# Last two scatters issued together, the low halves of w1 last in each tile's products, two loads of w2 after the transposes, and more products of zeros early

## The chip, the cores and the metric

One core of one Trainium2 chip runs the kernel. The metric is device microseconds (us) of one execution. The engines are TensorE (PE, with its weight loads as PEld), VectorE (DVE), ScalarE (ACT), GpSimd (POOL) and SyncE (SP), which here only issues transfers.

## The reference, cut to what matters

Three layers run one after the other on 2 x 768 tokens of 384 numbers: a recurrent attention, a gated convolution network, and a mixture of eight experts. Only the last one is touched by most of the change:

```python
logits = x @ w_gate                      # which of 8 experts a token asks for
fresh  = argmax(logits)                  # a token takes it only if its local gate is < 0.5,
e      = fresh or the expert of the token before it
out[b, s] = p[e] * (relu(x[b, s] @ w1[e]) @ w2[e])      # w1: 384 x 1024, w2: 1024 x 384
```

## The kernel before, in words

Each engine's order is written out by hand. The string `SEQ` (L50 on) is a list of tokens; every token names a small generator and advances it by one `yield`, and what is emitted stands in that order in the queue of its engine. PE, DVE, ACT and SP keep it as written; POOL is tied to program order too. So a token that is moved changes what waits behind it on its engine.

Every fp32 matrix is split into two fp16 halves, a high one and a low one (w1 into `w1h` and `w1l`, w2 into `w2h` and `w2l`), and a product is three products: high x high, high x low, low x high (`PASSES`).

**Early.** PE begins with products of zeros, `warm` (token H, L235 to 240: 128x512 fp16, tile `psk`). H_1 and H_2 are the first 16, H_0 are 8 more after the first states `psu` (L397). Between them come the transposes of tables (`psT`, L305) and of the first keys (`ptf`, L326 and L341).

**Routing.** The twelve tiles of 128 tokens go through the second layer's output (`out_tile`, L660) and are scattered by POOL into `slots` in DRAM, one region for each expert (tokens S, `send`, L882). A row's place comes from the routing (`places_of`, tile `posb` for the last two tiles, `xrb` their rows). The first full tiles of the sorted list, U_0_0 to U_0_2, are known before the last two scatters: their rows are gathered first (`fetch`, tokens I, L956), transposed by a DMA from SP (`xsT<-yb`, L973) and multiplied. Then come scatters S_11 and S_10. Everything else reads `slots` after both: tiles with a fixed expert straight from there (`xsT<-slots`, L975), all others through gathers on POOL and transposes on SP.

**Experts, first half of w1 and w2 (phase 0).** Tokens W1_e_0 and W2_e_0 load 768 KB of an expert into one of three staging buffers `ws` from SP (L932, L946). ACT writes the high half (L498), and the low half is written by DVE (L155), or for the experts that `CFG['w1']` marks with `g` by POOL (three instructions L153, after ACT has scaled `ws` in place, L937, and cast it, L939). Experts 6, 5, 7, 3, 0, 4, 2, 1 come in this order. Tokens U are `up` (L1023): 9 products into `ph`, 18 for a tile of two halves. Where the expert is only known at run time, the weight is addressed by a register that PE loads from `ej`/`ejs` (L997, L1005), and a product of `w1l` then waits for the low halves of all experts. After `up` come relu and split (L1011, L1013), a transpose on PE (`pt`, L1041) or by DMA, and later D, `down` (L1052), whose result goes to the output by scatters of POOL.

`F` computes on DVE the row numbers for all later gathers (L856 to L878), BL_1 and BL_2 blank the gather buffers on DVE (L964 to L966), `M` opens the memory that w2 uses. SP also loads one register from `ej` (L1104) at a place that the builder chooses.

Of the kernel before, what the change touches and what calls it, by code (L numbers as in the profile page):

```python
# [50 lines left out]
C LD H_1 H_1 C WI_0 CV LD C C C C C C C H_2 H_2 C C T T LD LD LD T T WO_0 WI_3 T T WI_0 LD L_3 LD LD A_0 CV A_0 A_0 A_0 T A_0 A_1 T C WI_0 T WI_0 WO_0  # L51
WO_0 WI_2 A_1 A_1 A_1 CV CV B_0 C B_0 B_0 Y_0 CV Y_0 L_3 WO_0 B_0 Z_0 Z_0 H_0 H_0 Z_1 Z_0 L_2 GT B_1 Y_0 A_1 Y_0 A_1 A_1 Y_1 L_2 B_1 GT L_2 L_2 A_2
WI_3 WI_3 Y_0 A_2 A_2 GT Y_0 Y_1 A_2 A_2 WI_1 Z_1 Z_2 Y_1 Y_1 Z_2 A_2 A_2 Y_2 WI_3 WO_1 L_3 L_3 A_3 A_3 A_3 WO_0 Y_0 Y_1 B_1 B_1 WO_0 Z_3 WI_1 Z_1 Y_1
Y_1 B_2 WO_0 Y_2 A_3 Y_2 B_2 B_2 A_3 WI_1 A_3 A_3 L_4 L_4 L_4 L_4 L_7 Z_2 WI_1 Y_0 Y_2 Y_2 A_4 B_3 Y_1 Y_1 G_0_0_1 A_4 L_5 CV CV WO_0 WI_2 G_0_0_1 B_2
G_0_0_1 A_4 Y_2 A_4 Z_3 Y_3 CV G_0_0_1 Y_3 L_5 L_5 L_5 B_3 Y_3 Y_2 WO_0 WO_0 WI_2 WI_2 B_3 WO_0 G_0_0_1 B_3 WO_2 Z_4 G_0_0_1 B_4 G_0_0_0 Y_2 Y_2 Z_3
G_0_0_1 WO_0 G_0_0_1 G_0_0_2 G_0_0_1 WO_1 A_4 G_0_0_2 WO_0 WO_0 WO_0 G_0_0_0 A_4 A_4 Z_4 Y_3 A_5 A_5 A_5 A_5 L_6 G_0_0_2 WO_1 A_5 Y_4 Y_4 L_6 L_6 L_6
A_6 A_6 G_0_0_1 Y_3 B_4 G_0_0_2 G_0_0_2 A_5 A_5 WO_1 Y_3 WO_3 G_0_0_0 WO_1 Y_4 G_0_0_0 G_0_0_2 G_0_0_2 G_0_0_2 G_0_0_2 A_6 A_6 B_4 Z_4 Y_4 Y_4 G_0_0_2
G_0_0_2 Y_3 G_0_0_0 Y_3 L_7 WO_2 Y_3 WO_1 WO_1 WO_1 A_6 G_0_0_0 WO_1 G_0_0_0 G_0_0_0 B_4 Y_4 WO_2 Y_5 Y_5 G_0_0_2 L_7 L_7 G_0_1_2 A_7 Y_5 G_0_1_2
G_0_1_2 G_0_1_2 G_0_1_2 G_0_0_0 G_0_1_1 B_5 B_5 B_5 WO_1 WO_1 WO_1 WO_1 Y_5 Y_5 WO_1 WO_1 A_7 A_7 A_6 A_6 G_0_1_2 G_0_1_2 G_0_1_2 G_0_1_1 A_6 G_0_1_1
WO_2 G_0_0_0 B_6 L_8 WO_2 G_0_1_1 B_6 WO_2 Y_4 G_0_1_2 G_0_1_1 G_0_1_1 G_0_1_1 G_0_1_2 A_7 B_5 G_0_1_1 G_0_1_0 Y_4 G_0_1_0 A_6 A_6 Z_6 Z_6 L_10  # L60
G_0_1_2 B_6 G_0_1_0 G_0_1_0 G_0_1_0 WO_3 RC G_0_1_2 A_7 WO_2 L_8 WO_2 WO_2 G_0_1_1 WO_2 WO_2 G_0_1_1 A_7 Z_7 A_7 Y_6 Z_6 A_7 Y_5 G_0_1_3 WO_3 G_0_1_3
G_0_1_0 Y_6 Y_6 G_0_1_0 G_0_1_0 G_0_1_3 G_0_1_3 B_7 A_7 A_7 B_6 G_0_1_3 G_0_1_3 L_8 L_8 Y_5 Y_5 Y_5 G_0_0_3 G_0_0_3 Y_4 G_0_1_0 G_0_0_3 G_0_0_3
G_0_0_3 WO_2 WO_2 G_0_0_3 G_0_1_1 Y_6 WO_2 WO_2 L_9 L_9 Y_6 G_0_1_0 G_0_1_1 O_0_1 G_0_0_3 G_0_0_3 G_0_0_3 A_8 A_8 G_0_1_3 Z_7 B_7 G_0_0_3 B_7 WO_3
O_0_1 O_0_1 Y_7 WO_3 Y_7 G_0_2_0 G_0_0_3 G_0_0_3 A_8 G_0_2_0 G_0_1_3 G_0_2_0 Y_6 Z_7 G_0_1_3 Y_7 G_0_2_0 G_0_2_0 G_0_2_0 O_0_2 O_0_2 L_9 L_9 A_9 O_0_2
G_0_1_3 Z_8 Y_6 A_9 WO_3 B_8 WO_3 WO_3 G_0_2_0 G_0_2_0 WO_3 L_11 Z_6 G_0_1_3 Z_8 G_0_2_1 A_8 G_0_1_3 G_0_2_0 G_0_2_0 B_7 WO_3 WO_3 Y_7 Y_7 G_0_2_1
G_0_2_1 G_0_2_1 G_0_2_1 Z_9 A_8 SI G_0_2_0 G_0_2_2 Y_7 G_0_2_1 G_0_2_1 A_8 G_0_2_2 G_0_2_1 A_9 O_0_0 WO_3 WO_3 A_8 WO_3 WO_3 O_0_0 O_0_0 Y_7 A_9 B_8
# [20 lines left out]
OR_1_5 OR_1_5 OR_1_5 R_1_4_2 R_1_4_2 W1_4_0 W1_4_0 R_1_4_2 W1_1_0 W1_2_0 R_1_4_2 R_1_4_2 R_1_4_2 R_1_4_2 F F I_2 I_2 OR_1_4 OR_1_4 OR_1_4 OR_1_4
R_1_4_2 I_0 I_0 I_0 Q_1_4_2 Q_1_4_2 Q_1_4_2 I_1 I_1 I_1 S_11 S_11 W1_2_0 OR_1_4 OR_1_4 M M W2_1_0 W1_4_0 BL_2 BL_2 W1_1_0 W2_1_0 W1_1_0 VE VE U_0_1
W2_6_0 F U_0_0 U_0_0 S_10 S_10 W2_2_0 W2_2_0 I_10 BL_1 BL_1 I_3 I_3 I_3 U_0_0 I_4 U_0_1 U_0_1 U_0_2 U_0_2 U_0_2 I_4 I_4 U_0_0 U_0_1 U_0_3 EJ EJ V V
I_10 I_10 I_13 I_6 I_13 I_13 U_0_10 U_0_13 I_12 I_12 I_12 W2_6_0 I_7 I_11 I_11 I_11 U_0_2 U_0_10 W2_1_0 W2_6_0 U_0_1 U_0_2 U_0_3 U_0_10 U_0_10 U_0_0  # L90
I_9 I_9 I_9 U_0_13 U_0_13 U_0_11 U_0_11 U_0_11 U_0_3 W2_4_0 U_0_9 W2_5_0 I_7 U_0_9 U_0_10 U_0_13 U_0_12 U_0_12 U_0_12 U_0_11 I_6 I_6 I_6 W2_4_0 I_7
I_7 W2_2_0 U_0_13 U_0_4 W2_4_0 U_0_3 U_0_7 U_0_4 I_5 I_5 I_5 I_5 U_0_4 U_0_12 W2_5_0 W2_5_0 U_0_6 U_0_6 W2_7_0 U_0_9 W2_7_0 W2_7_0 U_0_9 U_0_11 W2_0_0
I_8 I_8 U_0_9 I_8 I_8 U_0_5 W2_3_0 W2_0_0 U_0_5 W2_0_0 ME W2_3_0 U_0_8 U_0_4 U_0_12 W2_3_0 W1_6_1 W1_6_1 ME D_0_3 D_0_3 D_0_4 D_0_10 D_0_10 W1_6_1
U_0_7 U_0_7 W1_3_1 W1_3_1 U_0_8 W1_7_1 D_0_4 W1_7_1 D_0_13 W1_3_1 ME W1_7_1 U_0_5 D_0_1 D_0_1 W1_1_1 W1_1_1 W1_1_1 D_0_11 D_0_11 U_0_7 U_0_6 D_0_2
# [1057 lines left out]
```

## Time and profile before

| | us |
|---|---|
| median of 3 runs | 360.82 (359.06 to 361.00) |
| the profiled execution's own time | 361.64 |
| its span, first to last instruction | 359.9 |
| PE busy | 318.2 (88% of the span) |
| DVE busy | 258.3 (72%) |
| ACT busy | 196.0 (54%) |
| POOL busy | 189.9 (53%) |
| mean granted clock of TensorE | 0.953 of full |

The own time is 1.74 above the span: it holds what lies before the first and after the last instruction. "Busy" counts instructions only; a DMA that SP issues is not SP's busy time. A row of the timeline gives start, length, engine, line, operation and count, and in brackets how long the engine stood idle before it and what ended that idle time. Times of the trace are from the span's start.

### The profile page before, as it was taken

The numbers are of one execution on the slowest core, as the hardware profiler recorded it, in microseconds if no ns is written. First come the engines' busy times: TensorE is split into PE (matmuls) and PEld (weight loads), VectorE is DVE, ScalarE is ACT, GpSimd is POOL, SyncE is SP. The second block draws the span as 40 slices with busy tenths as digits, with TensorE's granted clock in tenths as the row PEclk, the third lists the DMA queues.
The fourth block names the chain that finished last, engine by engine and source line by source line (L and its number), as shares of the span: only waits on it lengthen the run. The fifth ranks groups of instructions, "written<-read, shape, count | busy, mean of one in ns | idle before, by whom it ended". The sixth has DMA issues, their size and how long they took to land. (4 is left out here: it accounts for less than half of the span.)

```text
span 359.9 us, 7880 instructions
## 1 busy us (share of the span) xinstructions
PE 318.2 (88%) x2823; PEld 218.2 (61%) x2823; DVE 258.3 (72%) x494; ACT 196.0 (54%) x343; POOL 189.9 (53%) x229
## 2 busy tenths in 40 slices
...
GB/s 156 261 177 269 64 203 172 107 108 133 113 123 90 105 35 75 134 265 90 134 175 134 155 207 224 137 165 229 286 296 224 259 291 253 277 68 65 143 92 41
DMA packets 109744, 58.81 MB, mean 163 GB/s; under 512 B 90547, under 2 KB 99463, under 8 KB 109700
## 3 DMA queue, kind: packets, MB, share of 16 engines
...
## 5 line engine op out<-in xcount | busy, mean ns | idle before, releaser
L1030 PE MATMUL ph<-w1h,xsT 128*128 (+2 forms) x240 | 57.7, 392 | 12.0 <-issue 8.3
L882 POOL DMA_INDIRECT out_dram<-yb x14 | 13.8, 986 | 101.1 <-DVE yb L1061 96.5
L1052 PE MATMUL py<-w2h,hT 128*128 (+2 forms) x320 | 57.6, 327 | 0.6 <-DMA hT<-hr 0.6
L1030 PEld LDWEIGHTS <-xsT 128*64 128x64 f16 (+1 forms) x360 | 26.9, 107 | 45.6 <-issue 8.6
L613 PE MATMUL psh<-x1T,wi_h 128*128 128x258 f16 (+2 forms) x288 | 49.6, 273 | 1.0 <-DVE pl L770 0.6
L1052 PEld LDWEIGHTS <-hT 128*64 128x64 f16 (+1 forms) x480 | 34.5, 105 | 22.4 <-issue 3.6
L613 PE MATMUL psh<-x1T,wi_l 128*128 128x258 f16 (+2 forms) x144 | 39.3, 273 | 0.0
L1052 PE MATMUL py<-w2l,hT 128*64 128x384 f16 (+2 forms) x160 | 38.0, 326 | 0.0
L1030 PE MATMUL ph<-w1l,xsT 128*128 (+2 forms) x120 | 35.0, 391 | 2.5 <-DVE wd L856 2.3
L660 PE MATMUL psx<-wo_h,g_h 128*128 128x393 f16 (+2 forms) x144 | 36.2, 279 | 0.9 <-ACT hp L618 0.6
L660 PE MATMUL psx<-wo_l,g_h 128*128 128x393 f16 (+2 forms) x144 | 36.5, 280 | 0.0
L660 PE MATMUL psx<-wo_h,g_l 128*128 128x393 f16 (+2 forms) x144 | 36.0, 279 | 0.0
L155 DVE SCALAR_TENSOR_TENSOR w2l<-ws,w2h 128x1536 f16<-128x1536 f32 x16 | 27.9, 1754 | 10.8 <-ACT w2h L498 10.7
L1011 ACT ACTIVATE hr<-ph 128x512 f16<-128x512 f32 x28 | 16.3, 598 | 33.8 <-PE ph L1030 25.5
L1013 DVE SCALAR_TENSOR_TENSOR hr<-ph,hr 128x512 f16<-128x512 f32 x28 | 18.7, 685 | 22.3 <-ACT hr L1011 22.3
L153 POOL TENSOR_TENSOR g_l<-cv,g_h 128x512 f16<-128x512 f32 (+2 forms) x31 | 30.2, 982 | 8.3 <-ACT g_h L164 7.8
L155 DVE SCALAR_TENSOR_TENSOR w1l<-ws,w1h 128x1536 f16<-128x1536 f32 x12 | 24.6, 2053 | 9.6 <-ACT w1h L498 9.6
L613 PEld LDWEIGHTS <-wi_h 128*128 128x128 f16 x288 | 27.1, 98 | 6.6 <-issue 0.6
L660 PEld LDWEIGHTS <-g_h 128*128 128x128 f16 x288 | 22.5, 99 | 12.8 <-issue 2.4
L498 ACT ACTIVATE w2h<-ws 128x1536 f16<-128x1536 f32 x16 | 23.7, 1483 | 11.9 <-DMA ws<-in_moe_w_dram 11.9
L618 ACT ACTIVATE hp<-psh 128x258 f32<-128x258 f32 (+2 forms) x47 | 17.9, 381 | 16.4 <-PE psh L613 15.4
L452 PE MATMUL psy<-vt,am 128*128 128x48 f32 x192 | 24.6, 284 | 0.0
...
## 6 DMA issues: line engine op xcount, KB each, us to landing
...
out_dram<-yb POOLq DMA_INDIRECT x14, 3.3
```

What stands on the lines that cost most here:

```text
L153: eng.tensor_tensor(out=lo, in0=src, in1=hi, op=ALU.subtract)
L155: nc.vector.scalar_tensor_tensor(out=lo, in0=src, scalar=scale, in1=hi, op0=ALU.mult, op1=ALU.subtract)
L452: nc.tensor.matmul(psy[:, h], lhsT=ams[h % 2][:, h // 2], rhs=vt[:, h], start=(h == 0), stop=(c == 0 and h == H - 1))
L498: nc.scalar.activation(out=hi, in_=src, func=AF.Copy, scale=scale)
L613: nc.tensor.matmul(ps[:, 0:n], lhsT=x[:, kk, ft * P:(ft + 1) * P], rhs=x1T[b][:, y, t0:t0 + n], start=(i == 0), stop=(i == 3 * NK - 1))
L618: nc.scalar.activation(out=hp[:, a, o:o + n], in_=ps[:, 0:n], func=AF.Relu, scale=2.0 ** -8)
L660: nc.tensor.matmul(ps[:, c0:c1], lhsT=x[part][:, ft, o:o + P], rhs=y[:, ft, c0:c1], start=(n == 0), stop=(n == 3 * NF - 1))
L882: q = nc.gpsimd.indirect_dma_start(out=dst, out_offset=bass.IndirectOffsetOnAxis(ap=idx.bitcast(U32), axis=0), in_=src, in_offset=None, bo ...
L1011: nc.scalar.activation(out=hi, in_=ps, func=AF.Relu)
L1013: nc.vector.scalar_tensor_tensor(out=lo, in0=ps, scalar=0.0, in1=hi, op0=ALU.max, op1=ALU.subtract)
L1030: nc.tensor.matmul(ps[hs], lhsT=W["xsT"][i][:, x * NK + kk, hs], rhs=part(W[("w1h", "w1l")[y]], o + kk * HF, HF), start=(n == 0), stop=(n ...
L1052: nc.tensor.matmul(ps[hs], lhsT=hT[:, x * KF + ft, hs], rhs=part(W[("w2h", "w2l")[y]], o + ft * DM, DM), start=(n == 0), stop=(n == 3 * KF ...
```

## The change

- `CFG['w1']`: expert 4's low half of w1 in phase 0 is written by DVE (one L155) instead of POOL (three L153), and ACT has one instruction for it instead of two.
- `up`: the nine products run over `kk` inside the pass, passes with `w1h` first, those with `w1l` last.
- `SEQ`: S_10 stands right after S_11 on POOL; W2_6_0 and W2_2_0 are loaded by SP behind the four transposes from `slots` instead of ahead of them.
- `warm`: H_0 has 16 products instead of 8; a new H_3 of 12 stands between the transposes of the tables and the first `ptf` of L341. A branch for `k_ >= NPSB`, which no token used, goes.

```diff
 CFG = {
...
-    'w1': 'vvvvgggg',
+    'w1': 'vvvvvggg',
...
 SEQ = """
...
+WI_0 LD L_3 LD LD A_0 CV A_0 A_0 A_0 T A_0 A_1 T C WI_0 T H_3 H_3 WI_0 WO_0 WO_0 WI_2 A_1 A_1 A_1 CV CV B_0 C
...
+OR_1_4 OR_1_4 S_10 S_10 M M W1_4_0 W2_1_0 BL_2 BL_2 W1_1_0 W2_1_0 W1_1_0 VE VE U_0_1 F U_0_0 U_0_0 I_10 BL_1 BL_1 I_3 I_3 I_3 U_0_0 I_4 U_0_1 U_0_1 U_0_2
+U_0_2 U_0_2 I_4 I_4 W2_6_0 W2_2_0 U_0_0 U_0_1 U_0_3 EJ EJ V V I_10 I_10 I_13 I_6 I_13 I_13 U_0_10 U_0_13 I_12 I_12 I_12 W2_6_0 W2_2_0 I_7 I_11 I_11 I_11
...
+    WARM = (16, 8, 8, 12)
+
     def warm(k_):
 
-        ps = psB.tile([P, 512], F32, name="psk", tag="m") if k_ < NPSB else st["ps1"].tile([P, 512], F32, name="psk", tag="ph")
-        for _ in range(8 if k_ < NPSB else 4):
+        ps = psB.tile([P, 512], F32, name="psk", tag="m")
+        for _ in range(WARM[k_]):
             nc.tensor.matmul(ps, lhsT=still[:, 0:P], rhs=still, start=True, stop=True)
         yield
...
-        for kk in range(NK):
-            for x, y in PASSES:
+        for x, y in sorted(PASSES, key=lambda p_: p_[1]):
+            for kk in range(NK):
                 for o, hs in offs:
```

POOL, from the gathers for the first three tiles on (`yb` with `rows_145`), before and then changed; `slots<-xrb` are S_11 and S_10, the last rows are gathers for later tiles:

```order
L956 DMA yb_2292<-slots,rows_145 128x392 x3
L882 DMA slots<-xrb,posb 12288x392
L153 TENSOR_TENSOR w1l<-ws,w1h 128x512 x3
L882 DMA slots<-xrb,posb 12288x392
L956 DMA yb_3228<-slots,rows 128x392 x2
```

```order
L950 DMA yb_2313<-slots,rows_145 128x392 x3
L876 DMA slots<-xrb,posb 12288x392 x2
L950 DMA yb_3251<-slots,rows 128x392 x2
L950 DMA yb_3250<-slots,rows 64x392
L950 DMA yb_3251<-slots,rows 128x392
```

The three instructions for expert 4 between the two scatters are gone.

DVE at the same place, before and then changed; `w1l` are the low halves of experts 2 and 1 (before) and 2, 4 and 1 (changed), `xrb<-psx` are the rows of the tile that S_10 sends, the memsets are BL_2:

```order
L155 SCALAR_TENSOR_TENSOR w1l<-ws,w1h 128x1536
L155 SCALAR_TENSOR_TENSOR xrb<-psx,xrb 128x384
L964 MEMSET yb_3228 128x5x384
L965 MEMSET yb_3228 128x5
L966 MEMSET yb_3228 128x5x7
L155 SCALAR_TENSOR_TENSOR w1l<-ws,w1h 128x1536
```

```order
L147 SCALAR_TENSOR_TENSOR w1l<-ws,w1h 128x1536
L147 SCALAR_TENSOR_TENSOR xrb<-psx,xrb 128x384
L147 SCALAR_TENSOR_TENSOR w1l<-ws,w1h 128x1536
L958 MEMSET yb_3251 128x5x384
L959 MEMSET yb_3251 128x5
L960 MEMSET yb_3251 128x5x7
```

Expert 4's low half now stands ahead of the memsets.

SP, from the last transpose for the first three tiles on, before and then changed; `ws` are loads of w2, `xsT<-slots` the fixed-expert tiles U_0_3 and U_0_4, the `xsT<-yb` after them U_0_10, U_0_13 and further tiles:

```order
L946 DMA ws<-in_moe_w_dram 128x4x384 x3
L975 DMA_TRANSPOSE xsT_2296<-slots 128x6x64 x2
L975 DMA_TRANSPOSE xsT_2297<-slots 128x6x64 x2
L973 DMA_TRANSPOSE xsT_2303<-yb_3228 128x6x128
L973 DMA_TRANSPOSE xsT_2306<-yb_3228 128x6x128
L973 DMA_TRANSPOSE xsT_2305<-yb_3228 128x6x128
L1104 TENSOR_LOAD ej
L1104 ISA x2
```

```order
L940 DMA ws<-in_moe_w_dram 128x4x384
L969 DMA_TRANSPOSE xsT_2317<-slots 128x6x64 x2
L969 DMA_TRANSPOSE xsT_2318<-slots 128x6x64 x2
L940 DMA ws<-in_moe_w_dram 128x4x384 x2
L1098 TENSOR_LOAD ej
L1098 ISA x2
L967 DMA_TRANSPOSE xsT_2324<-yb_3251 128x6x128
L967 DMA_TRANSPOSE xsT_2327<-yb_3251 128x6x128
```

Two loads moved from ahead of the transposes from `slots` to behind them, and so ahead of U_0_10's; the register load moved from behind the third of the transposes from `yb` to ahead of the first.

## Rows read from the trace of the kernel before

**Rows 1.** Who PE waited for, 234 to 262 us (total, times, longest).
```profile
PE ph L1030 <- DMA xsT<-yb: 1.5, 2, 0.8
PE ph L1030 <- DMA xsT<-slots: 0.7, 1, 0.7
```

**Rows 2.** Timeline of PE, 200 to 262 us (start, length; idle before it).
```profile
214.43 0.59 PE L1030 MATMUL ph<-w1h,xsT 128*128 x1 [5.76 <-issue]
217.27 0.59 PE L1030 MATMUL ph<-w1l,xsT 128*128 x1 [2.25 <-DVE wd L856]
...
233.42 0.38 PE L1030 MATMUL ph<-w1h,xsT 128*128 x1 [2.57 <-issue]
...
261.38 0.48 PE L1052 MATMUL py<-w2h,hT 128*64 128x384 f16 x2
```

**Rows 3.** Who PE waited for, 262 to 352 us, the longest.
```profile
PE py L1052 <- DMA hT<-hr: 0.6, 1, 0.6
```

**Rows 4.** Timeline of PE, 0 to 40 us.
```profile
14.55 0.66 PE L341 MATMUL ptf<-id,full 128*128 128x128 f32 x4 [3.51 <-POOL full L149]
...
17.72 2.61 PE L239 MATMUL psk<-still 128*128 128x512 f16 x8
22.64 0.88 PE L397 MATMUL psu<-vt,full 128*48 128x48 f32 x16 [2.31 <-DVE z L403]
```

**Rows 5.** Stretches: length, PE, PEld, DVE, ACT, POOL busy, granted clock, DMA.
```profile
11.10:14.50 3.40, 0.00 (x0) 0.00 (x0) 3.33 (x7) 2.78 (x5) 0.99 (x2) 1.00 0.98 348
22.70:32.80 10.10, 10.10 (x75) 9.36 (x77) 7.63 (x10) 4.06 (x8) 8.93 (x8) 0.50 0.85 221
```

**Rows 6.** Timeline of POOL, 195 to 219 us.
```profile
195.54 2.61 POOL L882 DMA_INDIRECT slots<-xr,posi  x1 [0.30 <-issue]
...
211.08 1.04 POOL L882 DMA_INDIRECT slots<-xrb,posb  x1 [3.20 <-ACT w1h L498]
212.15 3.37 POOL L153 TENSOR_TENSOR w1l<-ws,w1h 128x512 f16<-128x512 f32 x3
215.68 2.35 POOL L882 DMA_INDIRECT slots<-xrb,posb  x1 [0.17 <-issue]
```

**Rows 7.** Timeline of DVE, 195 to 221 us.
```profile
195.56 1.74 DVE L155 SCALAR_TENSOR_TENSOR w1l<-ws,w1h 128x1536 f16<-128x1536 f32 x1
...
210.16 1.66 DVE L964 MEMSET yb<- 128x1920 int32 x1 [0.37 <-DMA yb<-slots,rows]
...
211.80 5.34 DVE L155 SCALAR_TENSOR_TENSOR w1l<-ws,w1h 128x1536 f16<-128x1536 f32 x1
...
220.44 0.18 DVE L874 TENSOR_TENSOR rows<-la,lb 128x19 int32<-128x19 f32 x1
```

**Rows 8.** Timeline of SP's queue, 211 to 262 us (time spent issuing).
```profile
211.49 6.04 SPq L946 DMA_DIRECT2D ws<-in_moe_w_dram  x3
223.02 5.10 SPq L975 DMA_TRANSPOSE xsT<-slots  x4
228.35 11.20 SPq L973 DMA_TRANSPOSE xsT<-yb  x5
239.66 1.08 SPq L946 DMA_DIRECT2D ws<-in_moe_w_dram  x2
240.82 3.12 SPq L973 DMA_TRANSPOSE xsT<-yb  x2
```

**Rows 9.** Issue to landing: tile posb's two scatters; then the output's, from the page.
```profile
DMA to landing us min/median/max: 5.1/6.2/7.3
...
out_dram<-yb POOLq DMA_INDIRECT x14, 3.3
```

**Rows 10.** Issue to landing of tile xsT's transposes, 222 to 234 us.
```profile
DMA to landing us min/median/max: 2.5/3.5/4.4
```

**Rows 11.** The same, 240 to 241.5 us: the one transpose issued there.
```profile
DMA to landing us min/median/max: 7.0/7.0/7.0
```

**Rows 12.** Line L1104, the register that SP loads from ej.
```profile
L1104 SPq TENSOR_LOAD <-ej x1: 851/851/851, 235.1 to 235.1; - x1
```

More of the change, by code (lines that the diff above doesn't have):

```diff
@@ L50 @@
 SEQ = """
[L51 to L66, printed above, removed]
@@ L87 @@
[L87 to L94, printed above, removed]
@@ L99 @@
[L99 to L102 removed]
+C LD H_1 H_1 C WI_0 CV LD C C C C C C C H_2 H_2 C C T T LD LD LD T T WO_0 WI_3 T T
@@ new lines @@
+WI_0 LD L_3 LD LD A_0 CV A_0 A_0 A_0 T A_0 A_1 T C WI_0 T H_3 H_3 WI_0 WO_0 WO_0 WI_2 A_1 A_1 A_1 CV CV B_0 C
+B_0 B_0 Y_0 CV Y_0 L_3 WO_0 B_0 Z_0 Z_0 H_0 H_0 Z_1 Z_0 L_2 GT B_1 Y_0 A_1 Y_0 A_1 A_1 Y_1 L_2 B_1 GT L_2 L_2 A_2 WI_3
+WI_3 Y_0 A_2 A_2 GT Y_0 Y_1 A_2 A_2 WI_1 Z_1 Z_2 Y_1 Y_1 Z_2 A_2 A_2 Y_2 WI_3 WO_1 L_3 L_3 A_3 A_3 A_3 WO_0 Y_0 Y_1 B_1 B_1
+WO_0 Z_3 WI_1 Z_1 Y_1 Y_1 B_2 WO_0 Y_2 A_3 Y_2 B_2 B_2 A_3 WI_1 A_3 A_3 L_4 L_4 L_4 L_4 L_7 Z_2 WI_1 Y_0 Y_2 Y_2 A_4 B_3 Y_1
+Y_1 G_0_0_1 A_4 L_5 CV CV WO_0 WI_2 G_0_0_1 B_2 G_0_0_1 A_4 Y_2 A_4 Z_3 Y_3 CV G_0_0_1 Y_3 L_5 L_5 L_5 B_3 Y_3 Y_2 WO_0 WO_0 WI_2 WI_2 B_3
@@ new lines @@
+WO_0 G_0_0_1 B_3 WO_2 Z_4 G_0_0_1 B_4 G_0_0_0 Y_2 Y_2 Z_3 G_0_0_1 WO_0 G_0_0_1 G_0_0_2 G_0_0_1 WO_1 A_4 G_0_0_2 WO_0 WO_0 WO_0 G_0_0_0 A_4 A_4 Z_4 Y_3 A_5 A_5 A_5
+A_5 L_6 G_0_0_2 WO_1 A_5 Y_4 Y_4 L_6 L_6 L_6 A_6 A_6 G_0_0_1 Y_3 B_4 G_0_0_2 G_0_0_2 A_5 A_5 WO_1 Y_3 WO_3 G_0_0_0 WO_1 Y_4 G_0_0_0 G_0_0_2 G_0_0_2 G_0_0_2 G_0_0_2
+A_6 A_6 B_4 Z_4 Y_4 Y_4 G_0_0_2 G_0_0_2 Y_3 G_0_0_0 Y_3 L_7 WO_2 Y_3 WO_1 WO_1 WO_1 A_6 G_0_0_0 WO_1 G_0_0_0 G_0_0_0 B_4 Y_4 WO_2 Y_5 Y_5 G_0_0_2 L_7 L_7
+G_0_1_2 A_7 Y_5 G_0_1_2 G_0_1_2 G_0_1_2 G_0_1_2 G_0_0_0 G_0_1_1 B_5 B_5 B_5 WO_1 WO_1 WO_1 WO_1 Y_5 Y_5 WO_1 WO_1 A_7 A_7 A_6 A_6 G_0_1_2 G_0_1_2 G_0_1_2 G_0_1_1 A_6 G_0_1_1
```

60 lines of the change are left out of this document (32 added, 28 removed).

## The prediction

> **What bounds the kernel now.** I read the waits of PE first, then PE's timeline where they lie, then the queues that release them. After 262 us PE has one wait worth the name, 0.6 us [rows 3], so what arrives early at 262 arrives early at the end. The stretch to look at is the handover from routing to experts. There PE stands idle for 5.76 us before its first expert product at 214.43, then 2.25 us after that single product, and 2.57 us before U_0_10 at 233.42 [rows 2]; 1.5 and 0.7 us more follow up to 262, all for transposes [rows 1]. The 5.76 lie behind gathers and transposes that the change doesn't touch. The 2.25 are put down to DVE's L856, but DVE was in the `w1l` that ended at 211.80 + 5.34 = 217.14 [rows 7], and the second product of the old order reads `w1l`. What releases U_0_3 and everything later is the second scatter: it starts only at 215.68, behind POOL's three L153 [rows 6], and SP's transposes from `slots` start at 223.02 [rows 8], 7.3 us after it [rows 9].
>
> **The early products.** H_3 puts 12 products into a gap of 3.51 us, H_0 adds 8 ahead of one of 2.31 us [rows 4]. Eight took 2.61 us [rows 4], 0.33 each, so 12 take up to 3.9 and the second eight 2.6: at worst 0.4 + 0.3 = 0.7 us too long. The granted clock in the first gap was 1.00 [rows 5], so they should be shorter, and I cost them at nothing: POOL's and DVE's work, for which PE waits in both gaps, hides them; without that cover they cost the 0.7. Can they give something? From 22.7 to 32.8 the grant was 0.50, the 1.2 GHz level, with PE busy throughout. But POOL was busy 8.93 of those 10.10 us [rows 5], so at most 1.2 us could go. The idle 2.31 us just ahead of the stretch stays, since DVE sets its end, and I expect the clock to fall as before: 0.
>
> **Expert 4 on DVE.** POOL loses 3.37 us [rows 6], ACT one instruction that nobody waits for. DVE gains one L155 of 1.74 us [rows 7]. It stands before the memset, which began at 210.16: the rows of S_10's tile are done before that, so I put it at 209.8 to 211.5, the memset to 213.25, and the last `w1l` to 215.0. This holds if that one takes 1.75 instead of 5.34, which I take because POOL's 3.37 us lay inside the 5.34 and 1.74 + 3.37 = 5.1. The row numbers on DVE come 2.1 us earlier, 218.3 instead of 220.44 [rows 7], in time for gathers that can't start before the scatters have landed.
>
> **Low halves last.** The first tile's six `w1h` products run at once from 214.43. At half clock they last until about 217.0, and the low halves are there at 215.0, so the 2.25 us wait goes and the three tiles end some 2.5 to 3 us earlier. By itself this is worth nothing, for the next thing is U_0_3, which waits for the scatters.
>
> **The scatters together.** S_11 begins at 211.08 as before, since it waits for the gathers. Now DVE's new `w1l` runs until 211.5, and a scatter is held by it: the one of 215.68 ran to 218.03, 0.9 after DVE's L155 had ended, the one of 195.54 to 198.15, 0.85 after, against 1.04 for one beside the memset [rows 6, 7]. So S_11 ends near 212.4 and S_10 starts at 212.7. It is held again from 213.25 to 215.0 and ends near 215.6, 2.4 us earlier than before. Landing: before it was 7.3 - 2.35 = 5.0 and 5.1 - 1.04 = 4.1 us after the end, with loads of w2 in flight; output scatters land 3.3 - 0.98 = 2.3 after theirs [rows 6, 9] (0.98 is the common length of a scatter, 1.04 in the row). Two of the three loads now come later, so I take 3.0: landed at 218.6, against 223.0. Bounds 2.3 to 5.0.
>
> Here a rule speaks for a shorter time. A scatter of 195.54 started 0.02 us ahead of DVE's L155 and was still the one that lasted 2.61, while DVE needed its usual 1.74 [rows 6, 7]. The Trainium skill, page "SBUF — State Buffer", section "Who interferes with whom", says that DVE and GpSimd take a shared pair of ports by issue order, and the second one blocks fully. By that rule S_10, started at 212.7 before the last `w1l`, would end at 213.7 and be 1.9 us ahead of my sum; this trace's rows don't show it, and I go by the rows.
>
> **Two loads of w2 behind the transposes.** On SP: four transposes from 218.6, 5.10 us [rows 8], to 223.7; the two loads, 1.08 [rows 8], to 224.8; the register load, 0.85 [rows 12] with some 0.4 around it, to 226.1. Before, it stood behind the third transpose and fell into a wait. Then U_0_10's transpose is issued at 226.1, against 228.35 [rows 8]. From issue to U_0_10's product it was 233.42 - 228.35 = 5.07 us. But now 1.5 MB of loads stand directly ahead of it in the same queue. The nearest row is 240.82, issued 1.16 us after two such loads: it landed after 7.0 us, against the usual 3.5 [rows 8, 10, 11]. Here the loads have a lead of 2.4 us, so I add 3.5 - (2.4 - 1.16) = 2.25 (bounds 0 and 3.5). U_0_10 starts at 226.1 + 5.07 + 2.25 = 233.4: just where it was. So the 4.4 us won at the scatter are spent before PE sees them, all but what follows.
>
> What follows: in the old kernel SP handed out the five transposes in 11.20 us, since it waited for gathers, and reached the next loads at 239.66 [rows 8]. Now the gathers are 4 us earlier, the five need about 1.25 each and end near 232.4, and the next two loads and the transposes of the half tiles go out some 6 us earlier. So I let the later waits, 1.5 + 0.7 = 2.2 us [rows 1], go. The loads of w2 are no later for it: two come 8 us later, the next two 6 us earlier, and w2 is first read at 261.38 [rows 2].
>
> **Sum.** Early products 0, U_0_10 0, later waits -2.2: 261.38 becomes 259.2, and the own time 361.64 becomes 359.4. The profiled execution lies 0.82 above the median of the runs shown, so the median should be 358.6 against 360.82.
>
> **Rivals.**
> - *The gain is larger.* S_10 isn't held by DVE (1.9 us), or the loads don't delay U_0_10's transpose (2.25 us). For it: ordinary landings of 2.5 to 4.4 us [rows 10]; against: rows 11 and the scatter of 195.54. With one of the two, U_0_10 starts 1.9 to 2.25 us earlier: about 356.5. The early clock staying at 1.00 would be worth up to 1.2 of the same sort.
> - *The win stops at SP.* U_0_10 starts as before, and the later waits stay because the DMA queue is full rather than late. For it: four loads and nine transposes crowd into 224 to 240. Then all that is left is a few tenths: 360.4.
> - *Slower: the loads ahead of the five transposes.* U_0_10's transpose lands 7.0 us after its issue and the half tiles' behind the next loads likewise. U_0_10 starts at 226.1 + 5.07 + 3.5 = 234.7, 1.25 us later than before, with the waits of rows 1 still there: 362.1. It decides from a landing of 5.75 us on, if those waits stay; if they go, only from 8 us on. Over 0.5% it would need 0.6 us more than the 7.0 of rows 11.
> - *The change doesn't do what it says early.* The products of zeros run at the lower clock and overrun by 0.7: 359.3, inside the forecast.
>
> **Chances.** Forecast 0.5 (own range 357.5 to 359.7), larger gain 0.2, stops at SP 0.2, slower 0.1. About 0.5%, 1.8 us, is what a measurement of this kernel can tell from no change. The line for faster is 359.0: all of the larger gain and seven tenths of the forecast lie beyond it, 0.55. Of the slower case some two thirds stay within 1.8 us, and a few hundredths come from mishaps in the forecast, so slower has 0.06 and the same 0.39. The range takes in a larger gain with both of its parts partly there at the low end, and the mild end of the slower case: 355.8 to 361.2.
>
> **What would show it.** Right: a second scatter beginning near 212.7 and landing near 218.6; no wait of PE on `w1l` at 217; transposes from `slots` near 218.6; U_0_10's first product within 1 us of 233.4, its transpose landing more than 5 us after issue; w2's first product near 259. Wrong: S_10 ending near 213.7; U_0_10 before 231.5; a wait of PE before w2's first product, or grants of 1.00 between 23 and 33 us.

## The result, and the profile after

The changed kernel is **slower by 1.0%**: 364.46 us (median of 4 runs, 364.01 to 365.61) against 360.91 (4 runs, 359.06 to 361.74), a ratio of 1.0105, 95% interval 1.0064 to 1.0145. The forecast was 358.6, and the range ended at 361.2. The profiled execution took 365.61 us, with a span of 363.9 and a mean granted clock of 0.947. A ratio leaves out executions that are over 1.5% above the fastest of their kernel, and since that keeps only 2 of 12 for `h1` and 6 of 13 for `h2` below, the median of all executions stands beside the ratios there.

Line numbers of the changed kernel are 8 lower up to L234 (L155 is L147) and 6 lower behind it: `up` is L1024 now, the loads of w2 are L940, the transposes L967 (from `yb`) and L969 (from `slots`), the scatters L876, the gathers L950. The timeline of PE, as [rows 2] show it for before:

```profile
212.21 2.72 PE L1024 MATMUL ph<-w1h,xsT 128*128 x6 [5.17 <-DVE yb L960]
...
234.93 2.72 PE L1024 MATMUL ph<-w1h,xsT 128*128 x6 [11.34 <-issue]
...
260.70 0.38 PE L1024 MATMUL ph<-w1h,xsT 128*64 x1 [2.09 <-DMA xsT<-yb]
262.56 1.69 PE L1024 MATMUL ph<-w1h,xsT 128*64 128x512 f16 x11 [1.48 <-DMA xsT<-slots]
...
265.01 0.83 PE L1046 MATMUL py<-w2h,hT 128*64 128x384 f16 x2
```

Three points say where the time went. The first expert product (212.21) is 2.22 us earlier than before, U_0_10's (234.93) is 1.51 later, w2's first (265.01) 3.63 later, and the span ends 4.0 later. From the first product to U_0_10's it was 19.0 us before and is 22.7 now; from there to w2 it was 28.0 and is 30.1. The wait of 2.25 us for `w1l` is gone; ahead of U_0_10 PE stands idle for 11.34 us, where it was 2.57.

POOL, for [rows 6], and DVE, for [rows 7]:

```profile
208.60 2.13 POOL L876 DMA_INDIRECT slots<-xrb,posb  x1 [3.25 <-DVE xrb L147]
211.04 1.01 POOL L876 DMA_INDIRECT slots<-xrb,posb  x1 [0.30 <-issue]
217.90 1.05 POOL L950 DMA_INDIRECT yb<-slots,rows  x1 [5.86 <-DVE ej L872]
```

```profile
208.07 1.75 DVE L147 SCALAR_TENSOR_TENSOR w1l<-ws,w1h 128x1536 f16<-128x1536 f32 x1
...
211.80 1.72 DVE L147 SCALAR_TENSOR_TENSOR w1l<-ws,w1h 128x1536 f16<-128x1536 f32 x1
```

The second scatter ended at 212.05 instead of 218.03, 6 us earlier, and the gathers begin 6 us earlier. SP's queue, for [rows 8]:

```profile
209.01 0.52 SPq L940 DMA_DIRECT2D ws<-in_moe_w_dram  x1
216.48 5.09 SPq L969 DMA_TRANSPOSE xsT<-slots  x4
221.67 1.08 SPq L940 DMA_DIRECT2D ws<-in_moe_w_dram  x2
223.86 14.50 SPq L967 DMA_TRANSPOSE xsT<-yb  x5
238.47 1.07 SPq L940 DMA_DIRECT2D ws<-in_moe_w_dram  x2
```

All is 6.5 us ahead at 216.48 (223.02 before) and 4.5 ahead at 223.86 (228.35), and then the five transposes take 14.50 us instead of 11.20. The first of them is U_0_10's; tile `xsT`, 223 to 224.5 us:

```profile
L967 SPq DMA_TRANSPOSE xsT<-yb x1: 1602/1602/1602, 223.9 to 223.9; - x1
...
  PE ph L1024: 11.3, 1
...
DMA to landing us min/median/max: 9.1/9.1/9.1
```

It landed 9.1 us after its issue, where [rows 10] have 2.5 to 4.4 and [rows 11] 7.0. PE's row for U_0_10 names "issue", but the load of its weights (PEld), which reads `xsT` first, names the transpose; changed, then before:

```profile
233.03 0.10 PEld L1024 LDWEIGHTS <-xsT 128*128 128x128 f16 x1 [9.92 <-DMA xsT<-yb]
231.38 0.10 PEld L1030 LDWEIGHTS <-xsT 128*128 128x128 f16 x1 [1.01 <-DMA xsT<-yb]
```

From there to U_0_10's product it takes 1.9 us, and took 2.0 before. The gathers of the same stretch are no better (tile `yb`, POOL, 217 to 232.5 us):

```profile
L950 POOL DMA_INDIRECT yb<-slots,rows x9: 942/1012/2440, 217.9 to 229.7; - x9
...
DMA to landing us min/median/max: 3.9/8.7/10.0
```

The stretches show what the DMA engines did; the last two columns are their busy share and GB/s. Changed, then before:

```profile
216.00:218.00 2.00, 2.00 (x11) 0.93 (x10) 1.60 (x10) 0.07 (x1) 0.10 (x1) 1.00 0.07 14
218.00:222.00 4.00, 3.77 (x33) 2.10 (x33) 3.41 (x10) 1.68 (x3) 3.08 (x4) 1.00 0.60 121
222.00:224.00 2.00, 1.59 (x15) 0.60 (x11) 1.38 (x1) 0.00 (x0) 2.00 (x1) 1.00 0.89 126
224.00:228.00 4.00, 0.00 (x0) 0.00 (x0) 0.00 (x0) 0.46 (x1) 3.08 (x4) 0.77 1.04 362
228.00:230.00 2.00, 0.00 (x0) 0.00 (x0) 0.94 (x1) 1.03 (x1) 1.39 (x3) 0.50 1.39 202
230.00:234.00 4.00, 0.00 (x0) 0.10 (x1) 0.82 (x1) 1.48 (x1) 1.63 (x1) 0.50 1.25 128
```

```profile
218.00:222.00 4.00, 4.00 (x14) 1.55 (x13) 3.49 (x17) 0.68 (x1) 0.04 (x1) 0.68 0.97 337
222.00:224.00 2.00, 2.00 (x11) 0.90 (x10) 1.18 (x4) 0.85 (x2) 0.07 (x1) 1.00 0.33 119
224.00:228.00 4.00, 2.24 (x21) 1.19 (x18) 2.30 (x7) 3.58 (x4) 3.08 (x4) 1.00 0.57 118
228.00:234.00 6.00, 2.71 (x20) 1.31 (x21) 2.72 (x2) 0.00 (x0) 5.39 (x3) 1.00 0.69 143
```

Before, loads filled 218 to 222 while the second scatter's rows were on their way, and the gathers and transposes after 222 found the DMA engines a third to two thirds busy. Now the engines stand nearly idle at 216 to 218 (0.07), and the two loads, issued from 221.67 on and landed at 227.6 and 230.7 (5.9 and 8.4 us after issue), run in the middle of the gathers and of U_0_10's transpose. PE did nothing from 224 to 234, and its granted clock fell to 0.50, the 1.2 GHz level: U_0_10's first six products take 2.72 us; a tile that starts at 246.43, at the full clock, takes 1.46 for the same. (Before, the grant was down to 0.57 at 234 to 238, so this is only in part new.)

### The profile page after: what moved, and what is told of

Its sections match the earlier page's. It is cut to its first block, busy times and chain, and to the rows that moved or that the text cites. A ratio compares the mean times of both kernels' runs of the same rounds, so it can differ in the third digit from the quotient of the medians.

```text
span 363.9 us, 7915 instructions
## 1 busy us (share of the span) xinstructions
PE 320.9 (88%) x2843; PEld 217.1 (60%) x2843; DVE 256.1 (70%) x495; ACT 194.5 (53%) x342; POOL 185.8 (51%) x226
## 5 line engine op out<-in xcount | busy, mean ns | idle before, releaser
L876 POOL DMA_INDIRECT out_dram<-yb x14 | 13.8, 987 | 111.4 <-DVE yb L1055 110.2
L1024 PE MATMUL ph<-w1h,xsT 128*128 (+2 forms) x240 | 45.2, 397 | 20.3 <-issue 11.3
L1046 PE MATMUL py<-w2h,hT 128*128 (+2 forms) x320 | 58.7, 332 | 0.3 <-DMA hT<-hr 0.3
L1024 PEld LDWEIGHTS <-xsT 128*64 128x64 f16 (+1 forms) x360 | 27.0, 108 | 51.6 <-DMA xsT<-yb 16.2
L607 PE MATMUL psh<-x1T,wi_h 128*128 128x258 f16 (+2 forms) x288 | 50.2, 275 | 0.6 <-DVE pl L764 0.6
L1046 PEld LDWEIGHTS <-hT 128*64 128x64 f16 (+1 forms) x480 | 35.6, 107 | 22.3 <-issue 3.2
L147 DVE SCALAR_TENSOR_TENSOR w2l<-ws,w2h 128x1536 f16<-128x1536 f32 x16 | 28.0, 1754 | 19.1 <-ACT w2h L492 19.1
L1046 PE MATMUL py<-w2l,hT 128*64 128x384 f16 (+2 forms) x160 | 38.9, 331 | 0.0
L145 POOL TENSOR_TENSOR g_l<-cv,g_h 128x512 f16<-128x512 f32 (+2 forms) x31 | 30.1, 979 | 8.4 <-ACT g_h L156 8.0
L1005 ACT ACTIVATE hr<-ph 128x512 f16<-128x512 f32 x28 | 16.2, 598 | 26.6 <-PE ph L1024 22.4
L147 DVE SCALAR_TENSOR_TENSOR w1l<-ws,w1h 128x1536 f16<-128x1536 f32 x13 | 22.7, 1750 | 8.4 <-ACT w1h L492 8.4
L1024 PE MATMUL ph<-w1l,xsT 128*128 (+2 forms) x120 | 25.2, 404 | 0.0
L446 PE MATMUL psy<-vt,am 128*128 128x48 f32 x192 | 23.0, 273 | 0.0
```

Of the source, the lines that this page charges most:

```text
L145: eng.tensor_tensor(out=lo, in0=src, in1=hi, op=ALU.subtract)
L147: nc.vector.scalar_tensor_tensor(out=lo, in0=src, scalar=scale, in1=hi, op0=ALU.mult, op1=ALU.subtract)
L446: nc.tensor.matmul(psy[:, h], lhsT=ams[h % 2][:, h // 2], rhs=vt[:, h], start=(h == 0), stop=(c == 0 and h == H - 1))
L607: nc.tensor.matmul(ps[:, 0:n], lhsT=x[:, kk, ft * P:(ft + 1) * P], rhs=x1T[b][:, y, t0:t0 + n], start=(i == 0), stop=(i == 3 * NK - 1))
L876: q = nc.gpsimd.indirect_dma_start(out=dst, out_offset=bass.IndirectOffsetOnAxis(ap=idx.bitcast(U32), axis=0), in_=src, in_offset=None, bo ...
L1005: nc.scalar.activation(out=hi, in_=ps, func=AF.Relu)
```

## The experiments

The theory (Q below) was that the two loads, where they stand now, hold up the gathers and transposes behind them. Every kernel was compared with the one before on the same chip. On these chips single executions spread far more than in the result above (29 of the kernel before, on the last one: 357.99 to 365.05).

All kernels are read in the same way, from PE's timeline: first expert product, U_0_10's first product, and the first product that reads w2 (us):

| kernel | first | U_0_10 | w2 | first to U_0_10 | U_0_10 to w2 | both |
|---|---|---|---|---|---|---|
| before | 214.43 | 233.42 | 261.38 | 19.0 | 28.0 | 47.0 |
| before, `g4` | 213.49 | 233.29 | 263.24 | 19.8 | 30.0 | 49.8 |
| `e4` zeros only | 213.51 | 232.06 | 260.60 | 18.6 | 28.5 | 47.1 |
| `g3` low halves only | 212.49 | 232.51 | 261.12 | 20.0 | 28.6 | 48.6 |
| changed | 212.21 | 234.93 | 265.01 | 22.7 | 30.1 | 52.8 |
| changed, `f1` | 213.58 | 238.46 | 266.47 | 24.9 | 28.0 | 52.9 |
| changed, `h2` | 214.71 | 242.21 | 269.58 | 27.5 | 27.4 | 54.9 |
| `e2` loads only | 219.07 | 245.58 | 272.26 | 26.5 | 26.7 | 53.2 |
| `f3` loads from ACT | 216.15 | 236.57 | 267.59 | 20.4 | 31.0 | 51.4 |
| loads back, `e1` | 216.44 | 235.53 | 262.97 | 19.1 | 27.4 | 46.5 |
| loads back, `f2` | 213.23 | 231.35 | 258.91 | 18.1 | 27.6 | 45.7 |
| loads back, `h3` | 214.95 | 233.33 | 260.81 | 18.4 | 27.5 | 45.9 |
| `e3` behind the five | 219.77 | 233.99 | 267.68 | 14.2 | 33.7 | 47.9 |
| `f4` spread | 215.69 | 231.93 | 264.65 | 16.2 | 32.7 | 49.0 |
| `g1` one each side | 212.43 | 231.31 | 262.58 | 18.9 | 31.3 | 50.2 |
| `h1` in pieces | 213.82 | 229.47 | 262.04 | 15.7 | 32.6 | 48.2 |
| `g2` no loads | 213.96 | 229.12 | 256.51 | 15.2 | 27.4 | 42.6 |

**The loads put back (`e1`, `f2`, `h3`), beside the changed kernel (`f1`, `h2`).** The edit, in the changed kernel:

```diff
-VE VE U_0_1 F U_0_0 U_0_0 I_10
+VE VE U_0_1 W2_6_0 F U_0_0 U_0_0 W2_2_0 W2_2_0 I_10
...
-I_4 I_4 W2_6_0 W2_2_0 U_0_0
+I_4 I_4 U_0_0
...
-I_12 I_12 I_12 W2_6_0 W2_2_0 I_7
+I_12 I_12 I_12 W2_6_0 I_7
```

> The changed kernel with one thing undone: W2_6_0 and W2_2_0 are loaded ahead of the four transposes from slots again, as before. Theory Q (the two loads of w2 stand ahead of U_0_10's transpose and of the gathers' rows, and make them land 5 us late): slots' transposes still go out near 216.5, U_0_10's near 222.8, it lands after some 4 us instead of 9.1, U_0_10 starts near 228 instead of 234.9, the waits of 2.1 and 1.5 us behind it shrink, and the time is 355.5 to 357.5. Rival G (the gathers, which now begin 6 us earlier, beside the transposes from slots, slow the transposes themselves; the loads are innocent): U_0_10's transpose still takes 8 us or more, U_0_10 starts at 233 or later, time 362.5 to 364.5. Rival L (the low halves last, or expert 4 on DVE, cost the time): 362 or more with U_0_10 early.

> The changed kernel itself, once more, beside the kernels that undo parts of it. From its first expert product to U_0_10's it needed 22.7 us (212.21 to 234.93), the kernel before 19.0 (214.43 to 233.42), the one with the loads put back 19.1 (216.44 to 235.53), the one with the loads behind the five transposes 14.2 (219.77 to 233.99). Theory Q (loads ahead of the five transposes): 22 to 24 us here again, and over 1% slower than the same kernel with the loads put back. Rival V (what separated the runs is the variation of the first 200 us from execution to execution, not the handover): within 0.5% of the kernel with the loads put back.

> The changed kernel with the loads ahead of the transposes from slots, as before, on the same chip as the changed kernel. Theory Q: 1 to 2% faster than the changed kernel and within 0.5% of the kernel before, 18.5 to 19.5 us from the first expert product to U_0_10's, and the second scatter lands 6 us after its end (three loads in flight), which eats what the scatter gained. Rival V: no difference to the changed kernel beyond 0.5%.

> The changed kernel once more, for its distance to the next kernel on one chip: ratio to the kernel before 1.009 to 1.015, 22 to 25 us from the first expert product to U_0_10's.

> The changed kernel with the two loads ahead of the transposes from slots again, for the same distance: ratio 0.999 to 1.006, 18 to 19.5 us from the first expert product to U_0_10's. If it isn't under the changed kernel's ratio by 0.5% or more, the loads' place isn't what made the change slower.

Measured, changed: `f1` 1.0134 (1.0068 to 1.0200), 364.06 us against 359.99; `h2` 1.0015 (0.9966 to 1.0063), but 364.32 against 360.57 over all executions. Loads back: `e1` 1.0004 (0.9954 to 1.0055), `f2` 1.0054 (1.0013 to 1.0095), 360.44, `h3` 1.0007 (0.9971 to 1.0043), 361.39. On the two chips that ran both, putting the loads back takes 3.6 and 2.9 us off the median, and the stretch from the first product to U_0_10's falls from 24.9 and 27.5 us to 18.1 and 18.4. The intervals of `f1` and `f2` overlap, and `h2`'s ratio doesn't tell it from the kernel before: by the line that the expectation of `h3` drew, 0.5% between the two ratios, the last chip doesn't show the loads' place (0.08%). Over all executions it does: seven of 13 of `h2` took over 364 us, one of 12 of `h3` and one of 29 of the kernel before. The traces of `f1` and `h2` are of long executions (366.75 and 370.41), but the changed kernel's own, at 365.61, has the long stretch too, 22.7 us, and the three with the loads back have 18.1 to 19.1. Together this puts the slowdown down to the loads' place; its size, 3 to 4 us, is known only roughly. `e1` missed its 355.5 to 357.5 by far (365.68, on a chip where the kernel before took 365.64): with the loads back the kernel isn't faster than before either. The reason shows in SP's queue of `f2`:

```profile
210.12 3.85 SPq L940 DMA_DIRECT2D ws<-in_moe_w_dram  x3
219.50 5.10 SPq L969 DMA_TRANSPOSE xsT<-slots  x4
```

S_10 ended at 212.10 there, and the transposes from `slots` go out 7.4 us later, where the changed kernel waited 4.4 (212.05 to 216.48). S_10's rows landed 8.4 us after their issue there (219.5), together with the second load (issued at 210.7, landed after 9.0), and after 5.4 us in the changed kernel. So each place costs something: ahead, the loads hold up the scatter, behind, the rows.

**The loads moved in the kernel before (`e2`).** The reverse edit, in the kernel before.

```diff
-VE VE U_0_1 W2_6_0 F U_0_0 U_0_0 S_10 S_10 W2_2_0 W2_2_0 I_10
+VE VE U_0_1 F U_0_0 U_0_0 S_10 S_10 I_10
...
-I_4 I_4 U_0_0 U_0_1 U_0_3
+I_4 I_4 W2_6_0 W2_2_0 U_0_0 U_0_1 U_0_3
...
-I_12 I_12 I_12 W2_6_0 I_7
+I_12 I_12 I_12 W2_6_0 W2_2_0 I_7
```

> The kernel before with one thing done: the two loads of w2 behind the four transposes from slots. Theory Q: slots' transposes stay at 223.0, the loads go out at 228.2, U_0_10's transpose at 230.5 with a landing of 8 to 10 us, U_0_10 starts at 238 to 240.5 instead of 233.4, time 364.5 to 368. Rival G: the loads cost their issue only, some 2 us at U_0_10 and less at the end: 361 to 362.5.

Measured: 1.0051 (1.0003 to 1.0098), 369.50 us over all executions against 365.64. Its profiled execution was its longest (374.96), but the handover is like the changed kernel's: 26.5 us to U_0_10, whose transpose landed after 11.1 us. The move alone makes the kernel before slower, without earlier scatters or another order of products, which speaks against rivals G and L.

**Without the two loads (`g2`).** 

```diff
-        s_ = stg.tile([P, KF, DM], F32, name="ws", tag="stage", bufs=3)
-        nc.sync.dma_start(out=s_, in_=w2[e, ph * HF:(ph + 1) * HF, :].rearrange("(k p) n -> p k n", p=P))
+        if (e, ph) in ((6, 0), (2, 0)):
+            s_ = st["w2_1"]
+        else:
+            s_ = stg.tile([P, KF, DM], F32, name="ws", tag="stage", bufs=3)
+            nc.sync.dma_start(out=s_, in_=w2[e, ph * HF:(ph + 1) * HF, :].rearrange("(k p) n -> p k n", p=P))
...
```

> The changed kernel without the two loads that it moves: w2 of experts 6 and 2 is made from the tile of expert 1, so these two experts' results are left out and 1.5 MB less is moved; everything else stands where it stood. Theory Q (the bytes of the two loads, on the DMA engines shared by all queues): U_0_10's transpose lands after 2.5 to 4.5 us instead of 9 to 13, U_0_10 starts 14 to 15.5 us after the first expert product, ratio to the kernel before 0.980 to 0.992. Rival G (the gathers and transposes, closer together since the scatters are, hold each other up without any load): 20 us or more, ratio 1.005 to 1.013.

Measured: 0.9913 (0.9877 to 0.9948), 356.92 us. Gathers and transposes stand as close together as in the changed kernel, and land as they used to; tile `xsT`, 223 to 224 us, `yb`, 217 to 232.5, and the five transposes in SP's queue (L972 and L955 are the transposes and gathers there):

```profile
L972 SPq DMA_TRANSPOSE xsT<-yb x1: 1227/1227/1227, 223.3 to 223.3; - x1
...
DMA to landing us min/median/max: 3.4/3.4/3.4
```

```profile
L955 POOL DMA_INDIRECT yb<-slots,rows x9: 942/995/3647, 218.5 to 231.4; - x9
...
DMA to landing us min/median/max: 2.6/3.2/5.7
```

```profile
223.31 9.92 SPq L972 DMA_TRANSPOSE xsT<-yb  x5
```

3.4 us for U_0_10's transpose instead of 9.1, 3.2 for the gathers instead of 8.7, 15.2 us to U_0_10. Rival G is out: it is the loads. The DMA engines in the stretch in which the changed kernel has its loads:

```profile
224.00:228.00 4.00, 1.63 (x16) 0.73 (x13) 3.67 (x6) 2.05 (x2) 3.69 (x2) 1.00 0.93 196
```

**The loads from ACT (`f3`).**

```diff
-        nc.sync.dma_start(out=s_, in_=w2[e, ph * HF:(ph + 1) * HF, :].rearrange("(k p) n -> p k n", p=P))
+        (nc.scalar if (e, ph) in ((6, 0), (2, 0)) else nc.sync).dma_start(out=s_, in_=w2[e, ph * HF:(ph + 1) * HF, :].rearrange("(k p) n -> p k n", p=P))
```

> The changed kernel with the two loads issued by ACT instead of SP, at the same place of the program, so that U_0_10's transpose isn't behind them in its own queue, while the bytes still move at the same time. If the order within SP's queue is what delays the transposes: U_0_10's transpose lands after 4 to 5 us, 16 to 18 us from the first expert product to U_0_10's, 1 to 1.5% faster than the changed kernel. If it is the shared DMA engines, whichever queue feeds them: 21 us or more, as the changed kernel.

Measured: 1.0103 (1.0029 to 1.0177), 364.42 us, like the changed kernel; 20.4 us to U_0_10, between the two expectations and nearer to the second. Tile `xsT`, the first two of the five transposes:

```profile
L967 SPq DMA_TRANSPOSE xsT<-yb x2: 1227/1700/2173, 225.6 to 226.9; - x2
...
DMA to landing us min/median/max: 10.4/10.4/10.4
```

The trace has the landing of the second one only, 10.4 us (10.7 in the changed kernel). U_0_10's product began 11.0 us after its transpose's issue at 225.57 (11.07 in the changed kernel, 14.5 in `f1`). Neither load is ahead of them in SP's queue. So what remains of the delay, 5.2 us of stretch against `g2`'s 15.2, lies in what all queues share. In `f1`, on the same chip, it is 9.7; whether the other 4.5 us are the queue's or the spread of single executions isn't shown. The Trainium skill, page "DMA: Bandwidth & Descriptors", section "Issuing engines are not separate DMA queues", says that transfers issued by ScalarE, SyncE or GpSimd run interleaved on the same 16 DMA engines; the 10.4 us agree with it.

**Other places (`e3`, `f4`, `g1`, `h1`).** In the changed kernel the two loads go behind the five transposes (`e3`); there as well, with W2_4_0 and W2_5_0 behind the half tiles' first transposes (`f4`); W2_6_0 ahead of the transposes from `slots` and W2_2_0 behind the five (`g1`); in four pieces each, six of the eight singly between the transposes and two behind the five (`h1`). The heart of `e3`, then of `h1`:

```diff
-I_9 I_9 I_9 U_0_13 U_0_13 U_0_11 U_0_11 U_0_11 U_0_3 W2_4_0
+I_9 I_9 I_9 W2_6_0 W2_2_0 U_0_13 U_0_13 U_0_11 U_0_11 U_0_11 W2_6_0 W2_2_0 W2_6_0 U_0_3 W2_4_0
```

```diff
-        nc.sync.dma_start(out=s_, in_=w2[e, ph * HF:(ph + 1) * HF, :].rearrange("(k p) n -> p k n", p=P))
-        yield
+        n_ = 1 if (e, ph) in ((6, 0), (2, 0)) else KF
+        for k_ in range(0, KF, n_):
+            nc.sync.dma_start(out=s_[:, k_:k_ + n_], in_=w2[e, ph * HF + k_ * P:ph * HF + (k_ + n_) * P, :].rearrange("(k p) n -> p k n", p=P))
+            yield
```

> The changed kernel with the two loads moved on, behind the five transposes that begin with U_0_10's, so that nothing big is ahead of them. Theory Q: U_0_10's transpose goes out near 222, lands after 4 us, U_0_10 starts at 226.5 to 228.5; if w2 is still there in time (first w2 product at 256 to 258) the time is 355 to 357.5, if the loads come too late for it up to 360. Rival G: U_0_10 at 231 or later, 361.5 to 364.

> The changed kernel with the two loads behind the five transposes and the next two (W2_4_0, W2_5_0) behind the first transposes of the half tiles instead of ahead of them, so that no transpose up to there has loads just ahead of it. Theory Q: 14 to 15.5 us from the first expert product to U_0_10's and no wait of 4 us for the half tiles' rows (which the version with four loads in a row had), first w2 product 27 to 29 us after U_0_10, so 2 to 5 us less than the kernel before: a ratio of 0.987 to 0.995. If w2 then comes too late: waits of ACT or PE for w2 behind 260 us, ratio 1.00 or more.

> The changed kernel with W2_6_0 ahead of the transposes from slots, as before, and W2_2_0 behind the five transposes that begin with U_0_10's. Theory Q (the DMA engines are the bound of the handover, and a load costs its 2 us wherever rows are waited for): the scatters land 4.5 to 6 us after S_10's end instead of 7.4 with both loads there, U_0_10 starts 15.5 to 17.5 us after the first expert product (18.1 and 19.1 with both loads ahead, 22.7 and 24.9 as changed), and with one load less ahead of the half tiles their waits stay below 3 us: ratio to the kernel before 0.993 to 1.002. If instead the half tiles give all of it back: 1.003 to 1.01.

> The changed kernel with each of the two loads cut into four pieces of 192 KB that stand singly between the transposes from slots and the five after them. The bytes moved up to the half tiles are the same; no transpose has more than one piece just ahead of it. If large blocks ahead of a transpose are what costs: every transpose lands within 5 us, U_0_10 starts 16.5 to 19 us after the first expert product (0.5 us of issue for each piece included), ratio to the kernel before 0.995 to 1.004. If it is the sum of the bytes within the handover, however they are cut: U_0_10 after 20 us or more, or the half tiles late by as much, ratio 1.006 to 1.014.

Measured: `e3` 1.0118 (1.0038 to 1.0198), `f4` 1.0105 (1.0056 to 1.0155), `g1` 1.0059 (1.0021 to 1.0098). `h1` had two executions far below its others (355.68 and 358.96, the rest 362.09 to 365.90): its ratio of 0.9906 (0.9833 to 0.9979) rests on those two, and its median is 363.54 against 360.57. What set these two apart stays open. In all but `g1` U_0_10 comes early, after 14.2 to 16.2 us, as Q says, and in all four the stretch after it grows to 31.3 to 33.7 us, from 27.4 to 27.6 us with the loads back. PE's timeline of `h1` shows who waits there (`up` is L1026 in it):

```profile
229.47 2.38 PE L1026 MATMUL ph<-w1h,xsT 128*128 x6 [3.86 <-issue]
246.22 0.38 PE L1026 MATMUL ph<-w1h,xsT 128*64 x1 [1.34 <-DMA xsT<-yb]
247.36 1.48 PE L1026 MATMUL ph<-w1h,xsT 128*64 128x512 f16 x11 [0.76 <-DMA xsT<-slots]
258.23 3.12 PE L1026 MATMUL ph<-w1h,xsT 128*64 x12 [3.50 <-DMA xsT<-yb]
```

Now it is the half tiles' transposes that come late: PE waits 5.6 us for transposes from U_0_10 to w2, and 2.3 and 2.4 in `f2` and `h3`. In `f4` the 5.25 us before 257.76 are DVE's instead: the low halves of w2 stand ahead of `hr` on it and wait for ACT's casts, of which one waited 2.56 us for a load. So there my order of the casts and the loads' landing share the cost. No place paid: by the medians, no version that computes everything is clearly faster than the kernel before.

**The other parts (`e4`, `g3`, `g4`).**

```diff
-        for _ in range(8 if k_ < NPSB else 4):
+        for _ in range((16, 8, 8, 12)[k_]):
...
-A_0 A_1 T C WI_0 T WI_0 WO_0
+A_0 A_1 T C WI_0 T H_3 H_3 WI_0 WO_0
```

```diff
-        for kk in range(NK):
-            for x, y in PASSES:
+        for x, y in sorted(PASSES, key=lambda p_: p_[1]):
+            for kk in range(NK):
```

> The kernel before with one thing done: 16 products of zeros in H_0 and 12 in H_3. Theory E (they keep the granted clock at 1.00 between 16 and 33 us, and PE is 2.5 us ahead from there on, all of which reaches the end): 357.9 to 358.9, granted clock 1.00 from 22.7 to 32.8, first gather near 201.7. Rival N (the lead is lost again at the gathers, where SP, POOL and DVE set the time, or the clock fell for another reason): 360.2 to 361.2.

> The kernel before with one thing done: the three products with w1l last in each half tile. By the prediction's step the wait of 2.25 us for w1l shrinks to under 0.5 us, and nothing of it reaches the end, since U_0_3 waits for the scatters: ratio 0.997 to 1.003. If the order of the products cost something itself (weights loaded in another order, the clock falling in a longer wait behind them): over 1.005.

> The kernel before, to have its trace on the same chip: 18.5 to 19.5 us from the first expert product to U_0_10's, the scatter landing 5 us after its end, and a first gather within 3 us of the other kernels of this chip, whether they have the added zeros or not.

Measured: zeros alone 1.0004 (0.9971 to 1.0038), low halves alone 0.9998 (0.9956 to 1.0039); both are worth nothing. In the trace of the changed kernel the clock stayed at 1.00 between 16 and 33 us (0.60 before) and its first gather came at 201.69 instead of 204.23; I took that for a gain of 2.5 us (theory E), and it isn't one. On the chip of `f1` to `g4` the first gather came at 202.02, 202.81, 204.43, 204.27, 202.46 and 203.24 with the added zeros, and at 202.25 and 203.34 without; the grant from 16 to 33 us was between 0.80 and 1.00 with, 0.75 and 0.77 without. The lead was within what executions differ by.

## Why the prediction was wrong

By its own steps, on the profiled executions:

- **Early products, 0.** Right in the price (`e4`: 1.0004). That the clock falls held in eight of the twelve later traces with the added zeros; in the changed kernel's own and four others it stayed at 1.00. The 2.2 us that the changed kernel was ahead at the first product I take for chance; they hide part of its loss.
- **Expert 4 on DVE, low halves last.** Right. The last `w1l` took 1.72 us, no longer 5.34, the 2.25 us wait went, and it was worth nothing (`g3` for the low halves alone; the loads-back kernels, 1.0004 to 1.0054, for everything but the loads).
- **The scatters together.** Right in kind. S_10 took 1.01 us instead of the 2.9 I gave it, and the transposes from `slots` went out at 216.48 instead of 218.6, though 4.4 us after its end rather than 3.0, within the bounds of 2.3 to 5.0. Part of that lead is the same chance: S_11 began at 208.60 instead of 211.08. The half of the larger gain that rested on the rule of the Trainium skill, page "SBUF — State Buffer", section "Who interferes with whom" (issue order decides who is blocked), came true: S_10 began 0.76 us ahead of the last `w1l` and wasn't held; S_11 began 0.53 us after another and ended 0.91 us after it. The scatter of 192.99, recorded 0.02 us ahead of a `w1l`, took 2.61 us all the same, like the one of 195.54 before; why isn't shown. The rule decided nothing, since U_0_10 waits elsewhere.
- **Two loads behind the transposes: this step failed.** I added 2.25 us to U_0_10's transpose, with 3.5 as the upper bound, from one row (a landing of 7.0 us behind two loads). From issue to product it was 11.07 us instead of 5.07, so 6.0 more, and in `f1` 14.5 (223.94 to 238.46). The landing of 9.1 is past even the "slower" rival's 7.0. That rival named the right place and mechanism; its price was too low, and its chance of 0.1 as well.
- **The later waits, -2.2: failed, in the main for the same reason.** I let the five transposes end at 232.4, at 1.25 us each. But the gathers that they wait for landed after 8.7 us, where `g2` has 3.2, the five took 14.50 us, and the next loads went out at 238.47, 1.2 us earlier than before and not 6 (by my own 232.4 it should have read 7). The 1.25 was too low even without the loads: in `g2` the five took 9.92 us, since they wait for gathers there too. The waits of 1.5 + 0.7 us [rows 1] became 2.1 + 1.5.

The sum closes: against the forecast the stretch to U_0_10 is 3.7 us longer (22.7 for 19.0), the one after it 4.3 (30.1 for 25.8), the rest 0.4, less the 2.2 us of chance: 6.2, and the execution's own time is 365.61 where I had 359.4.

Behind both failed steps is one mistake. I treated the loads as two entries in SP's queue, with a lead of 2.4 us over the transpose. They are 1.57 MB for the DMA engines, by estimate 4.3 us of all of them at the 362 GB/s of 224 to 228, and the change took them out of a stretch that had little else to move than the second scatter's rows (0.97 busy at 218 to 222 before, 0.07 at 216 to 218 now) and put them where gathers, transposes and loads want the engines at once. The profile of before had shown this: 0.33 to 0.69 busy after 222 was the room in which the rows landed in 3.5 us.

What isn't settled is why the delay is larger than 4.3 us. Against `g2` U_0_10 lost 7.5 us (22.7 for 15.2), in `f1` and `h2` 9.7 and 12.3. In the changed kernel the engines are over 1.0 busy at 228 to 234, where the second load lands at 230.7, and move only 202 and then 128 GB/s, while `g2` moves 196 GB/s at a share of 0.93. What slows gathers and transposes once they have piled up wasn't taken apart; holding the gathers back wasn't tried.
